# A spectral filter plus a gated layer on one core: a new order, new engines and new PSUM banks for 998 planned tasks

## The chip, the cores and the metric

The kernel runs on one core of one Trainium2 chip. The metric is the device time of one launch in microseconds. The core has five engines with an instruction stream each: PE (TensorE, matmuls; its weight loads are listed as PEld), DVE (VectorE), ACT (ScalarE), POOL (GpSimd) and SP (SyncE, which here only issues DMAs). Each stream runs in its own order, and streams meet at semaphores.

## The reference

```python
def reference(A_x, A_w_r, A_w_i, B_x, B_w_gate, B_w_up, B_w_down):
    def _A_ref(x, w_r, w_i):                    # x (1, 2048, 640)
        X = rfft2(x.astype(float32), axes=(-2, -1))
        X = X * (w_r + 1j * w_i)                # (2048, 321)
        return irfft2(X, s=(S, D), axes=(-2, -1)).astype(bfloat16)
    def _B_ref(x, w_gate, w_up, w_down):        # (640, 1536) twice, (1536, 640)
        g = einsum("bsd,df->bsf", x, w_gate)
        u = einsum("bsd,df->bsf", x, w_up)
        return einsum("bsf,fd->bsd", g * u, w_down)
    xn = _layernorm(A_x, axis=-1)
    return A_x + _A_ref(xn, A_w_r, A_w_i) + _B_ref(xn, B_w_gate, B_w_up, B_w_down)
```

All arrays are bf16. So the output is the input, plus a two-dimensional Fourier filter of the normalized input, plus a bilinear gated layer (GLU) of it.

## The kernel before

The kernel is a list of 998 tasks. A task has a name, the engines that may run it, a planned duration for each, and a function that emits its instructions. `_PLAN` (L403) is a written-out table of triples: task number, engine (0 PE, 1 ACT, 2 DVE, 3 POOL, 4 SP) and, for a PE task that opens PSUM space, its first bank of eight. `replay` (L151) walks the table in order, gives each task to its engine's stream, and makes whoever takes a bank depend on the tasks that emptied it. `compute_waits` (L196) turns dependences into semaphore waits. The durations in the code enter only into the planned clock that `replay` keeps; the emitted program is set by the table's order, engines and banks. A task's instruction waits at the head of its engine's stream, and everything behind it on that engine waits too.

The work has three stages.

Stage A normalizes the 16 row blocks (bn, ag, sd, rs, mul or sm, sq), transposes them (T0 on PE for the first four blocks, with evictions eT0; DMA transposes xt for the others), runs the first GLU groups (GU, L945 and L965, five matmuls of 512 columns each, or ten narrower ones in the first), and makes a first transform on DVE (S1 to S5) and PE (R, L905, evicted by eR). Every GU pair is evicted to bf16 (eG, L688 on ACT or L689 on DVE) and multiplied on DVE (H, L981). The buffer between eG and H has three slots.

Stage B carries the spectrum for t = 0 to 15 while the remaining GLU groups run beside it:

- D_t_0 and D_t_1 (PE, L1021) read the first transform. eD copies each result from PSUM as two copies of 64 partitions, one of which crosses to the other partition half.
- C_t (PE, L1041) is two matmuls of 321 columns into a pair of banks.
- WM_t (DVE, L1058 and L1061) multiplies C's result by the filter, six instructions, 256 columns four times and 130 columns twice.
- For every odd t, SM_t (DVE, L1074 and L1075) adds products across the partition halves; JA_t and JB_t (L689/L688 and L1086/L1085) copy or negate its halves across.
- A small side branch does the same for the columns divisible by five: X5A (L1096 on POOL or DVE, L1095 on ACT) and X5B, then the sum S5M (L1105), then J5A and J5B (L1117 is J5B's negation).
- IA (PE, L1132), four for every odd t, read all of SM, JA, JB and S5M, J5A, J5B of that t. eIA evicts them.

Stage C turns back: I (PE, L1160) needs all IA, eI evicts it, V1 to V5 (DVE) finish the inverse transform for a group of rows. ACC (PE, L1237) accumulates the GLU's down projection in PSUM, IV (PE, L1249) adds the inverse transform into the same bank, FINA (ACT) evicts, FIN (DVE) adds the input, and st_out stores.

Four functions show what the moved tasks do:

```python
def copy_on(c, dst, src):                                   # L686
    if c.e is nc.scalar:
        return c.e.activation(dst, src, _ACTF.Copy)
    return c.e.tensor_copy(dst, src)
...
def em_sm(c, lr=lr):                                        # L1072
    pa_, pb_ = v_pr[:, 0], v_pr[:, 1]
    c.e.tensor_tensor(v_l[0:64, lr, :, 0, :], pa_[0:64], pb_[64:128], _OP.subtract)
    return c.e.tensor_tensor(v_l[64:128, lr, :, 0, :], pa_[64:128], pb_[0:64], _OP.add)
...
def em_x5b(c):
    return copy_on(c, v_x5[64:128, :, 0:65], v_y5[0:64, 1, :, 0:65])
...
def em_s5(c, lr=lr):                                        # L1104
    return c.e.tensor_tensor(v_l5[:, lr, :, 0:65], v_y5[:, 0, :, 0:65], v_x5[:, :, 0:65], _OP.add)
```

Of the kernel before, what the change touches and what calls it, by code (L numbers as in the profile page):

```python
# [398 lines left out]
def _d_act(n):  # L399
    return n * 0.833 + 62.0  # L400
# [3 lines left out]
    (11, 4, -1), (0, 1, -1), (12, 4, -1), (170, 1, -1), (169, 4, -1), (17, 2, -1), (171, 4, -1), (8, 3, -1), (18, 2, -1),  # L404
    (19, 2, -1), (26, 2, -1), (20, 1, -1), (172, 4, -1), (21, 2, -1), (22, 2, -1), (10, 0, 0), (27, 2, -1), (28, 2, -1),
    (29, 1, -1), (23, 0, 2), (24, 1, -1), (25, 2, -1), (9, 0, 4), (30, 2, -1), (31, 2, -1), (181, 0, 5), (13, 4, -1),
    (32, 0, 6), (34, 2, -1), (33, 1, -1), (179, 0, 4), (189, 0, 0), (186, 0, 1), (14, 4, -1), (182, 2, -1), (36, 2, -1),
    (184, 0, 5), (191, 0, 2), (180, 1, -1), (35, 2, -1), (37, 2, -1), (183, 2, -1), (173, 4, -1), (187, 2, -1), (43, 1, -1),
    (38, 1, -1), (174, 4, -1), (196, 0, 3), (44, 1, -1), (45, 1, -1), (39, 2, -1), (194, 0, 4), (185, 2, -1), (175, 4, -1),
    (190, 1, -1), (40, 2, -1), (192, 1, -1), (41, 0, 5), (195, 1, -1), (188, 2, -1), (46, 2, -1), (47, 2, -1), (197, 1, -1),  # L410
    (112, 2, -1), (42, 1, -1), (201, 0, 6), (193, 2, -1), (176, 4, -1), (15, 4, -1), (113, 2, -1), (48, 0, 7), (198, 2, -1),
    (199, 0, 1), (49, 1, -1), (114, 2, -1), (177, 4, -1), (178, 4, -1), (206, 0, 0), (204, 0, 7), (50, 2, -1), (1, 4, -1),
    (53, 2, -1), (202, 1, -1), (211, 0, 6), (200, 1, -1), (207, 1, -1), (203, 2, -1), (51, 2, -1), (16, 4, -1), (62, 1, -1),
    (63, 1, -1), (54, 2, -1), (52, 2, -1), (55, 2, -1), (212, 1, -1), (2, 4, -1), (205, 1, -1), (56, 1, -1), (115, 2, -1),
    (3, 4, -1), (208, 2, -1), (209, 0, 2), (57, 2, -1), (210, 1, -1), (216, 0, 4), (64, 1, -1), (116, 2, -1), (214, 0, 5),
    (65, 1, -1), (4, 4, -1), (221, 0, 3), (5, 4, -1), (58, 2, -1), (217, 1, -1), (213, 2, -1), (121, 2, -1), (219, 0, 2),
    (119, 0, 0), (6, 4, -1), (226, 0, 4), (66, 1, -1), (215, 1, -1), (222, 1, -1), (7, 4, -1), (67, 2, -1), (218, 2, -1),
    (117, 0, 6), (122, 2, -1), (60, 2, -1), (59, 4, -1), (224, 0, 5), (220, 1, -1), (68, 2, -1), (72, 1, -1), (123, 2, -1),
    (223, 2, -1), (229, 0, 3), (124, 2, -1), (73, 1, -1), (70, 2, -1), (74, 1, -1), (227, 1, -1), (61, 4, -1), (75, 1, -1),
    (225, 1, -1), (125, 2, -1), (76, 1, -1), (231, 0, 2), (77, 2, -1), (234, 0, 4), (232, 1, -1), (230, 1, -1), (236, 0, 5),  # L420
    (120, 1, -1), (126, 0, 2), (69, 4, -1), (228, 2, -1), (71, 4, -1), (239, 0, 0), (78, 2, -1), (118, 1, -1), (237, 1, -1),
    (79, 4, -1), (82, 1, -1), (80, 2, -1), (233, 2, -1), (130, 2, -1), (128, 0, 6), (235, 1, -1), (81, 4, -1), (83, 1, -1),
    (241, 0, 1), (238, 2, -1), (131, 2, -1), (244, 0, 5), (240, 1, -1), (246, 0, 4), (431, 4, -1), (84, 1, -1), (249, 0, 0),
    (242, 1, -1), (243, 2, -1), (432, 4, -1), (251, 0, 1), (85, 1, -1), (132, 2, -1), (247, 1, -1), (433, 4, -1), (92, 1, -1),
    (254, 0, 4), (245, 1, -1), (256, 0, 5), (252, 1, -1), (86, 1, -1), (248, 2, -1), (87, 2, -1), (250, 1, -1), (434, 4, -1),
    (93, 1, -1), (257, 1, -1), (94, 1, -1), (133, 2, -1), (255, 1, -1), (95, 1, -1), (253, 2, -1), (90, 2, -1), (259, 0, 1),
    (261, 0, 0), (435, 4, -1), (134, 2, -1), (266, 0, 5), (258, 2, -1), (96, 1, -1), (97, 2, -1), (262, 1, -1), (260, 1, -1),
    (264, 0, 4), (88, 2, -1), (98, 2, -1), (129, 1, -1), (269, 0, 0), (137, 0, 6), (271, 0, 1), (127, 1, -1), (436, 4, -1),
    (100, 2, -1), (135, 0, 2), (267, 1, -1), (270, 1, -1), (263, 2, -1), (437, 4, -1), (438, 4, -1), (102, 1, -1), (274, 0, 5),
    (265, 1, -1), (138, 1, -1), (439, 4, -1), (440, 4, -1), (276, 0, 0), (272, 1, -1), (143, 2, -1), (268, 2, -1), (275, 1, -1),  # L430
    (103, 1, -1), (144, 2, -1), (141, 0, 6), (139, 0, 4), (277, 1, -1), (281, 0, 1), (136, 1, -1), (282, 1, -1), (279, 0, 0),
    (273, 2, -1), (104, 1, -1), (145, 2, -1), (278, 2, -1), (286, 0, 1), (105, 1, -1), (284, 0, 2), (287, 1, -1), (146, 2, -1),
    (280, 1, -1), (106, 1, -1), (283, 2, -1), (140, 1, -1), (289, 0, 3), (291, 0, 1), (107, 2, -1), (294, 0, 0), (285, 1, -1),
    (296, 0, 2), (290, 1, -1), (441, 4, -1), (147, 2, -1), (292, 1, -1), (442, 4, -1), (148, 0, 4), (471, 4, -1), (142, 1, -1),
    (110, 2, -1), (288, 2, -1), (150, 0, 6), (472, 4, -1), (295, 1, -1), (108, 2, -1), (301, 0, 3), (293, 2, -1), (473, 4, -1),
    (89, 4, -1), (154, 0, 0), (297, 1, -1), (299, 0, 2), (302, 1, -1), (156, 2, -1), (91, 4, -1), (99, 4, -1), (298, 2, -1),
    (149, 1, -1), (157, 2, -1), (101, 4, -1), (151, 1, -1), (300, 1, -1), (306, 0, 3), (474, 4, -1), (303, 2, -1), (152, 0, 4),
    (304, 0, 2), (307, 1, -1), (153, 1, -1), (311, 0, 3), (305, 1, -1), (158, 2, -1), (309, 0, 2), (475, 4, -1), (155, 1, -1),
    (310, 1, -1), (308, 2, -1), (312, 1, -1), (476, 4, -1), (316, 0, 6), (159, 2, -1), (317, 1, -1), (477, 4, -1), (160, 2, -1),
    (319, 0, 7), (478, 4, -1), (313, 2, -1), (314, 0, 6), (167, 0, 4), (161, 0, 0), (320, 1, -1), (168, 1, -1), (315, 2, -1),  # L440
    (162, 2, -1), (163, 0, 2), (165, 0, 6), (164, 2, -1), (321, 0, 4), (166, 1, -1), (318, 2, -1), (445, 0, 5), (109, 4, -1),
    (446, 2, -1), (322, 1, -1), (111, 4, -1), (443, 0, 0), (451, 0, 1), (449, 0, 6), (429, 4, -1), (430, 4, -1), (723, 4, -1),
    (323, 2, -1), (444, 1, -1), (324, 0, 7), (450, 1, -1), (479, 0, 0), (724, 4, -1), (325, 1, -1), (447, 0, 2), (326, 0, 4),
    (480, 1, -1), (452, 2, -1), (507, 4, -1), (453, 0, 6), (485, 0, 5), (448, 2, -1), (329, 0, 1), (487, 0, 0), (481, 0, 2),
    (327, 1, -1), (334, 0, 4), (486, 1, -1), (331, 0, 3), (454, 2, -1), (488, 1, -1), (508, 4, -1), (459, 3, -1), (330, 1, -1),
    (458, 1, -1), (328, 2, -1), (515, 0, 5), (517, 0, 0), (455, 2, -1), (482, 1, -1), (336, 0, 1), (460, 3, -1), (335, 1, -1),
    (489, 0, 6), (509, 4, -1), (516, 2, -1), (553, 0, 2), (332, 1, -1), (333, 2, -1), (483, 0, 4), (337, 1, -1), (490, 2, -1),
    (339, 0, 3), (484, 2, -1), (554, 1, -1), (510, 4, -1), (511, 4, -1), (457, 1, -1), (344, 0, 1), (461, 3, -1), (341, 0, 2),
    (338, 2, -1), (521, 0, 6), (491, 2, -1), (340, 1, -1), (494, 3, -1), (518, 1, -1), (345, 1, -1), (523, 0, 7), (342, 1, -1),
    (346, 0, 3), (495, 1, -1), (343, 2, -1), (524, 1, -1), (496, 3, -1), (512, 4, -1), (492, 2, -1), (462, 3, -1), (513, 4, -1),  # L450
    (456, 2, -1), (498, 3, -1), (522, 1, -1), (551, 0, 2), (514, 4, -1), (543, 4, -1), (349, 0, 0), (519, 0, 4), (354, 0, 1),
    (347, 1, -1), (525, 0, 6), (552, 1, -1), (493, 1, -1), (520, 2, -1), (497, 3, -1), (469, 0, 3), (544, 4, -1), (356, 0, 2),
    (526, 2, -1), (355, 1, -1), (531, 3, -1), (348, 2, -1), (350, 1, -1), (545, 4, -1), (351, 0, 4), (499, 0, 5), (465, 0, 1),
    (357, 1, -1), (589, 0, 0), (557, 0, 2), (467, 0, 6), (470, 1, -1), (352, 1, -1), (558, 1, -1), (463, 0, 7), (546, 4, -1),
    (503, 0, 4), (361, 0, 3), (547, 4, -1), (500, 1, -1), (548, 4, -1), (530, 3, -1), (549, 4, -1), (559, 0, 2), (359, 0, 5),
    (550, 4, -1), (468, 1, -1), (532, 3, -1), (590, 2, -1), (353, 2, -1), (579, 4, -1), (527, 2, -1), (580, 4, -1), (466, 1, -1),
    (501, 0, 6), (560, 1, -1), (555, 0, 0), (364, 0, 2), (362, 1, -1), (504, 1, -1), (534, 3, -1), (358, 2, -1), (581, 4, -1),
# [66 lines left out]
def _build(nc, A_x, A_w_r, A_w_i, B_w_gate, B_w_up, B_w_down, out, opts=None):  # L524
# [3 lines left out]
    with es:  # L528
# [49 lines left out]
        b_pr = alloc("PR", 2048)  # L578
# [92 lines left out]
        T = sch.task  # L671
# [60 lines left out]
        for gi, (b0, nb) in enumerate(_LN_GROUPS):  # L732
            pbase = 1.0 + 0.05 * gi if gi < 4 else opts.get("ln_prio", 5.9) + 0.05 * (gi - opts.get("ln_lead", 3))
            for b in range(b0, b0 + nb):
                if b in aset:
# [9 lines left out]
                    def em_sq(c, b=b):  # L745
# [3 lines left out]
                      reads=[(b_x, ("s", b, b + 1)), (b_m32, ("b", b, b + 1))],  # L749
# [611 lines left out]
```

## Time and profile before

| what | value |
|---|---|
| median of 8 runs | 200.58 us (200.39 to 201.18) |
| the profiled execution's own time | 200.47 us |
| its span, first to last instruction | 198.7 us |
| granted TensorE clock | 1.0 throughout |
| busy share of the span | PE 97%, DVE 91%, ACT 72%, POOL 12% |
| instructions | PE 1593 matmuls, DVE 394, ACT 307, POOL 35 |
| first and last work | first LayerNorm statistics 3.32 us, last addition 196.43 us |

Times inside the execution are microseconds from the span's start. In a row of the groups, "busy" is the sum over the group and the next number the mean duration in ns. An instruction's duration includes the tail in which the next one already runs, so two neighbours may start closer together than the duration: where a start-to-start distance is meant, the text says so. A busy PE is not a PE at its peak.

### The profile page before, as it was taken

What the parts mean: (1) busy time and instruction counts of PE and PEld (TensorE: products, weight loads), DVE (VectorE), ACT (ScalarE), POOL (GpSimd) and SP (SyncE); (2) the same over time, 40 slices, a digit from 0 to 9 for tenths busy, and PEclk for the clock granted to TensorE, in tenths of its full rate; (3) what the DMA queues carried; (4) which work ended last, traced back from release to release, by engine and by line L of the source; (5) the groups of instructions that cost most, each with busy time, mean ns of one, the idle gap of its engine ahead of it and who ended that gap; (6) DMA issues with size and microseconds to landing.
All of it is one profiled execution on the core that took longest, in us unless ns stands there. A gap on an engine that the chain in (4) does not pass through costs nothing.

```text
span 198.7 us, 4239 instructions
## 1 busy us (share of the span) xinstructions
PE 192.6 (97%) x1593; PEld 122.3 (62%) x1593; DVE 180.6 (91%) x394; ACT 142.1 (72%) x307; POOL 23.1 (12%) x35
## 2 busy tenths in 40 slices
PE   8899999999999999899899999999999999999995
PEld 8798645445455555455455555457777777777774
DVE  3799999999999999999999999997999998999653
ACT  3398999999969589999898999998414431543220
POOL 0000000000000003184353442320000000000000
PEclk9999999999999999999999999999999999999999
DMA  6999995417327441442332400205101235033412
GB/s 184 306 330 376 387 163 115 126 35 109 95 47 228 163 115 46 108 113 63 96 88 58 122 0 3 68 0 147 54 3 47 85 102 162 36 132 102 132 68 68
DMA packets 29652, 23.26 MB, mean 117 GB/s; under 512 B 10560, under 2 KB 27584, under 8 KB 29504
## 3 DMA queue, kind: packets, MB, share of 16 engines
q1 hardware_dynamic: 28832, 22.64, 41.5%
q10 hardware_dynamic: 800, 0.36, 0.6%
q8 instruction: 12, 0.20, 0.5%
q14 instruction: 8, 0.07, 0.1%
HBM read 18.40 MB, written 2.62 MB: 106 GB/s over the span
## 4 chain that ended last, share of the span: by engine, by line
PE 77%; ACT 13%; DVE 6%; issue 1%; DMA 1%
PE ps L945 33%; PE ps L1237 26%; ACT arena L688 12%; PE ps L965 7%; PE ps L905 2%; PE ps L1160 2%; PE ps L1249 2%; DVE arena L1058 2%; PE ps L1132 1%; PE ps L1021 1%; DMA arena<-in_A_x_dram 1%; PE ps L1041 1%; DVE arena L689 1%; DVE arena L755 1%; DVE arena L981 1%
## 5 line engine op out<-in xcount | busy, mean ns | idle before, releaser
L688 ACT ACTIVATE arena<-ps 128x512 bf16<-128x512 f32 (+7 forms) x241 | 116.0, 531 | 46.1 <-PE ps L1249 24.6
L945 PE MATMUL ps<-arena 128*128 128x512 bf16 x420 | 98.2, 379 | 0.1
L945 PEld LDWEIGHTS ps<-arena 128*128 128x128 bf16 x420 | 38.6, 98 | 40.7 <-ACT arena L688 0.6
L1237 PE MATMUL ps<-arena 128*128 128x320 bf16 (+2 forms) x396 | 57.2, 295 | 0.0
L1237 PEld LDWEIGHTS ps<-arena 128*128 128x128 bf16 x396 | 37.6, 98 | 13.2
L1058 DVE TENSOR_TENSOR arena<-ps,arena 128x256 bf16<-128x256 f32 x64 | 22.6, 414 | 0.2
L981 DVE TENSOR_TENSOR arena<-arena 128x512 bf16<-128x512 bf16 x42 | 18.4, 440 | 0.4
L689 POOL COPY arena<-arena 64x252 bf16<-64x252 bf16 (+1 forms) x13 | 6.3, 487 | 92.3 <-DVE arena L1061 91.0
L965 PE MATMUL ps<-arena 128*128 128x128 bf16 (+1 forms) x160 | 14.0, 246 | 0.5 <-ACT arena L688 0.5
L965 PEld LDWEIGHTS ps<-arena 128*128 128x128 bf16 x160 | 12.3, 98 | 1.6 <-issue 0.6
L1276 DVE TENSOR_TENSOR arena<-arena 128x640 bf16<-128x640 bf16 x15 | 7.2, 489 | 6.2 <-ACT arena L688 5.9
L689 DVE CAST arena<-ps 64x321 bf16<-64x321 f32 (+4 forms) x20 | 10.6, 549 | 0.9 <-PE ps L945 0.4
L1021 PEld LDWEIGHTS ps<-arena 128*128 128x128 bf16 x160 | 7.4, 98 | 4.0 <-issue 0.4
L746 ACT ACTIVATE arena<-arena 128x640 bf16<-128x640 bf16 x11 | 9.3, 842 | 0.1
L1132 PEld LDWEIGHTS ps<-arena 128*128 128x128 bf16 x160 | 7.7, 116 | 2.5
L1041 PE MATMUL ps<-arena 128*128 128x321 bf16 x32 | 7.0, 300 | 2.0 <-ACT arena L688 1.2
L737 ACT ACTIVATE arena<-arena 128x640 bf16<-128x640 bf16 x11 | 8.3, 752 | 0.7 <-DMA arena<-in_A_x_dram 0.6
L1132 PE MATMUL ps<-arena 128*128 128x64 bf16 x160 | 8.6, 198 | 0.0
L1021 PE MATMUL ps<-arena 128*128 128x64 bf16 (+1 forms) x160 | 8.4, 193 | 0.0
L1249 PE MATMUL ps<-arena 128*128 128x320 bf16 (+2 forms) x33 | 8.1, 295 | 0.0
L1061 DVE TENSOR_TENSOR arena<-ps,arena 128x130 bf16<-128x130 f32 x32 | 7.9, 289 | 0.0
L857 DVE TENSOR_TENSOR arena<-arena 128x768 f32<-128x768 bf16 (+1 forms) x10 | 7.9, 790 | 0.0
(66 smaller groups left out, 199.3 us busy)
## 6 DMA issues: line engine op xcount, KB each, us to landing
arena<-in_A_x_dram SPq DMA_DIRECT2D x20, 160.0 KB, 2.6
arena<-in_A_w_r_dram SPq DMA_DIRECT2D x30, 80.2 KB, 2.2
arena<-in_A_w_i_dram SPq DMA_DIRECT2D x30, 80.2 KB, 2.2
out_dram<-arena SPq DMA_DIRECT2D x15, 160.0 KB, 1.8
arena<-in_B_w_gate_dram SPq DMA_DIRECT2D x4, 320.0 KB, 5.3
arena<-in_A_x_dram SPq DMA_DIRECT2D x1, 1280.0 KB, 9.9
arena<-in_B_w_down_dram SPq DMA_DIRECT2D x2, 640.0 KB, 7.1
arena<-c_tf SPq DMA_DIRECT2D x4, 256.0 KB, 10.1
```

The lines of the kernel that those rows point to most:

```text
L688: return c.e.activation(dst, src, _ACTF.Copy)
L689: return c.e.tensor_copy(dst, src)
L746: return c.e.activation(v_jk, v_x[:, b, :], _ACTF.Square, scale=-1.0, bias=v_m32[:, b:b + 1], accum_out=v_ss[:, b:b + 1])
L945: ins = c.e.matmul(ps[:, bk, :], v_gw[:, w, j, ft, :], v_xt[:, j, rows], start=(j == 0), stop=(j == 4))
L965: ins = c.e.matmul(ps[:, bk, w * n:(w + 1) * n], v_gw[:, w, j, ft, :], v_xt[:, j, rows], start=(j == 0), stop=(j == 4))
L981: return c.e.tensor_tensor(v_ht[:, ft0, rows], v_gbf[:, rr, 0, :], v_gbf[:, rr, 1, :], _OP.mult)
L1021: ins = c.e.matmul(ps[:, bk, k * 64:k * 64 + n], v_uq[:, k, t, :], v_fd[:, k * 128 + w * n: k * 128 + w * n + n], start=True, stop=True)
L1041: ins = c.e.matmul(ps[:, bank_of(c.t) + g, 0:_LP], v_tf[:, 2 * t + g, :], v_a[:, ar, 324 * g:324 * g + _LP], start=True, stop=True)
L1058: c.e.tensor_tensor(dst, xh, wv, _OP.mult)
L1132: ins = c.e.matmul(ps[:, bk, 64 * k:64 * k + 64], st, v_ti[:, q, :], start=True, stop=True)
L1237: ins = c.e.matmul(ps[:, bk, 0:sl3.stop - sl3.start], v_ht[:, ft, a * 128:(a + 1) * 128], v_wd[:, ft, sl3], start=(ft == _FT_ORDER[0]), st ...
L1249: return c.e.matmul(ps[:, bank_of(own), 0:sl3.stop - sl3.start], v_sm[:, 2, :], v_v[:, a, sl3], start=False, stop=True)
```

## The change

The whole table is replaced. The tasks, their instructions and their operands are the same 998; their order on PE, ACT, DVE and POOL, the engine of 31 of them, and the first bank of 213 of the 251 tasks that open PSUM space differ. SP's list and the two loads on ACT's queue stay as they were, in the same order.

In the code two kinds of lines differ: the table, of which two lines are shown here, and the planned durations.

```diff
-    (11, 4, -1), (0, 1, -1), (12, 4, -1), (170, 1, -1), (169, 4, -1), (17, 2, -1), (171, 4, -1), (8, 3, -1), (18, 2, -1),
...
+    (984, 2, -1), (994, 0, -1), (990, 2, -1), (985, 4, -1), (995, 0, -1), (991, 4, -1), (996, 2, -1), (997, 4, -1),
...
-                ed = T("eD_%d_%d" % (t, w), ("act", "dve"), {"dve": 910.0, "act": 880.0},
+                ed = T("eD_%d_%d" % (t, w), ("act", "dve"), {"dve": 1032.0, "act": 906.0},
...
-            wm = T("WM_%d" % t, "dve", 1862.0, em_wm,
+            wm = T("WM_%d" % t, "dve", 1800.0, em_wm,
...
-            T("SM_%d" % t, "dve", 1420.0, em_sm, reads=[(b_pr, ("r", 0, 2))],
+            T("SM_%d" % t, "dve", 1520.0, em_sm, reads=[(b_pr, ("r", 0, 2))],
...
-                T("%s_%d" % (nm, t), ("act", "dve"), {"act": _d_act(1024) + 70.0, "dve": 454.0}, em,
+                T("%s_%d" % (nm, t), ("act", "dve"), {"act": 1079.0, "dve": 500.0}, em,
...
-                T("%s_%d" % (nm, t), ("pool", "act", "dve"), {"pool": 950.0, "act": _d_act(260) + 20.0, "dve": 330.0}, em,
+                T("%s_%d" % (nm, t), ("pool", "act", "dve"), {"pool": (1250.0, 760.0)[i_], "act": 445.0, "dve": 330.0}, em,
...
-            T("S5M_%d" % t, ("pool", "dve"), {"pool": 900.0, "dve": 204.0}, em_s5,
+            T("S5M_%d" % t, ("pool", "dve"), {"pool": 1450.0, "dve": 332.0}, em_s5,
...
-                T("%s_%d" % (nm, t), ("pool", "act", "dve"), {"pool": 900.0, "act": _d_act(252) + 20.0, "dve": 330.0}, em,
+                T("%s_%d" % (nm, t), ("pool", "act", "dve"), {"pool": (620.0, 1240.0)[i_ - 1], "act": 440.0, "dve": 330.0}, em,
```

With names in place of numbers, the tasks that change engine are these.

| task | before to after |
|---|---|
| eT0_1_act, eR_14, eG_28_0 | ACT to DVE |
| eR_12, eR_13, eG_0_1, eG_27_0 | DVE to ACT |
| eD_4_0 | DVE to ACT |
| eG_43_0; eG_43_1, eG_47_0 | ACT to DVE; DVE to ACT |
| JB_1, JB_13 | ACT to DVE |
| X5A_1, X5B_11 | ACT to DVE |
| X5A_5 | POOL to DVE |
| X5A_3, X5A_9 | POOL to ACT |
| X5B_3, X5B_15 | ACT to POOL |
| S5M_9, S5M_13; S5M_15 | DVE to POOL; POOL to DVE |
| J5B_15 | DVE to ACT |
| eIA_25, eIA_28; eIA_30 | ACT to DVE; DVE to ACT |
| eI_0, eI_1, eI_11; eI_2 | ACT to DVE; DVE to ACT |

The order changes throughout. The places that matter for reading on are the starts of PE's and DVE's lists and the end of DVE's list in stage B:

```
PE  before: warm T0_0 fill GU_1_0 T0_1 GU_0_0 GU_0_1 GU_3_0 ...
PE  after:  warm T0_0 fill T0_1 GU_1_0 GU_0_0 GU_1_1 GU_3_0 ...
DVE before: bn0_0 bn0_1 ag0 bn1_0 rs_0 mul0 bn1_1 ag1 eT0_0_dve rs_1 mul1 eT0_1_dve eG_0_1 ...
DVE after:  bn0_1 bn0_0 bn1_1 ag0 bn1_0 rs_0 ag1 mul0 rs_1 mul1 eT0_0_dve eT0_1_dve eT0_1_act ...
DVE before, end of stage B: WM_15 WM_14 H_46 SM_15 JB_15 J5B_15 JA_15 eG_47_0 eIA_30 eIA_31 eG_48_1 eI_2 H_47 V1_0
DVE after,  end of stage B: WM_15 H_45 WM_14 H_46 SM_15 S5M_15 JA_15 JB_15 eIA_25 eIA_28 eIA_31 eG_48_1 eI_1 H_47 eI_0 V1_0
PE  before, end of stage B: GU_11_12_1 IA_30 IA_29 IA_31 IA_28 ACC_0_0_0
PE  after,  end of stage B: GU_11_12_0 IA_28 IA_29 IA_31 IA_30 ACC_0_0_0
```

On ACT the new list has `eIA_26 eIA_21 X5A_15 eG_47_0 eIA_24 J5B_15 eIA_27` near the end of stage B. The last eleven PE tasks are the same in both tables.

## The prediction

> **What bounds the kernel now.** I read the page's busy line and chain first, then busy time in windows, then the waits in one window, then single rows. The page points at two engines:
>
> ```profile
> PE 192.6 (97%) x1593; PEld 122.3 (62%) x1593; DVE 180.6 (91%) x394; ACT 142.1 (72%) x307; POOL 23.1 (12%) x35
> PE 77%; ACT 13%; DVE 6%; issue 1%; DMA 1%
> ```
>
> PE is busy and carries 77% of the chain, but 13% runs over ACT and 6% over DVE, so there is a stretch where PE follows. The chain in order of time puts it between 80 and 121 us. There are three stages. A, to 71.2 us: GLU matmuls and the first transforms. B, 71.2 to 135.1: D, C, WM, SM, JA/JB, IA beside 42 GLU groups. C, from 135.1: ACC, I, V, IV. In A (from 8.5) and C PE works without a gap. Busy us in five windows of B, columns PE, PEld, DVE, ACT, POOL:
>
> ```profile
> 71.50:80.00 8.50, 8.41 (x82) 4.45 (x79) 8.23 (x21) 8.23 (x19) 2.04 (x3) 1.00 0.38 102
> 80.00:92.00 12.00, 11.27 (x82) 5.66 (x83) 11.78 (x32) 11.70 (x24) 4.52 (x6) 1.00 0.37 90
> 92.00:105.00 13.00, 11.81 (x126) 6.91 (x124) 12.65 (x31) 12.29 (x30) 6.88 (x9) 1.00 0.38 96
> 105.00:121.00 16.00, 16.00 (x141) 8.57 (x139) 15.64 (x42) 15.17 (x34) 6.22 (x8) 1.00 0.19 48
> 121.00:134.00 13.00, 12.90 (x117) 6.84 (x116) 12.68 (x36) 12.75 (x29) 3.14 (x5) 1.00 0.10 27
> ```
>
> DVE and ACT are both near 97%. Which leads? The waits inside 71.5 to 134 us (total, times, longest), asked by engine:
>
> ```profile
> DVE arena L689 <- PE ps L1021: 0.2, 1, 0.2
> ACT arena L688 <- PE ps L945: 0.8, 2, 0.4
> ACT arena L688 <- PE ps L1021: 0.4, 1, 0.4
> PE ps L1041 <- ACT arena L688: 1.2, 2, 0.7
> PE ps L1041 <- DVE arena L689: 0.5, 1, 0.5
> ```
>
> DVE waits for others 0.2 us in 62.5. ACT and PE wait for it or for each other. So B is as long as DVE's own list, and PE's stalls there are the consequence. Their size: 42 groups x 1.079 us (start to start) + 16 C x 0.272 + 32 D x 0.145 + 32 IA x 0.166 = 59.6 us of PE work, against 135.09 - 71.22 = 63.9, so 4.2 us of stall. DVE's last item in B gates its end:
>
> ```profile
> 133.52 0.42 DVE L689 COPY arena<-arena 64x1024 bf16<-64x1024 bf16 x1
> 134.38 0.88 PE L1132 MATMUL ps<-arena 128*128 128x64 bf16 x20
> ```
>
> JA_15 ends at 133.94; the last four IA could start 0.15 us later (mul0 to T0_0 took that), at 134.09, and start at 134.38: 0.29 us to spare.
>
> **The change, part by part.** *Start.* DVE gets bn1_1 ahead of ag0 (start to start 0.41 us), so mul0 and T0_0 come 0.4 later. But T0_1 then runs before the first GLU group instead of after it, and PE's 0.15 us wait for eT0_1 ahead of the group at 8.49 is gone. Walked through: the later eT0 evictions end 6.89, the first group starts 7.14 instead of 6.95, yet without T0_1's 0.28 and the 0.15 behind it the third group starts 8.26 instead of 8.49: -0.2 us. In A, H_26 stands behind the same DVE work in both lists, and R_12 becomes ready as before. eR_12 and eR_13 go to ACT, eR_14 to DVE: three ACT evictions 0.58 apart end at about 70.85, and D_0_1 starts at 71.0 instead of 71.22. I take -0.2; ends 0 (A's DVE eats it) and -0.25. mul6 and mul7 swap, so xt6 and xt7 are issued up to 3 us later and land by about 33; their first reader stands at 35.
>
> *DVE's list in B.* Counting kinds from eD_0_1 to the last JA/JB: eD 4 to 3, JB 5 to 7, X5A 1 to 3, X5B 0 to 1, S5M 2 to 1, J5B 1 to 0; WM 16, SM 8, H 19, JA 6, eIA 1 and eG 1 stay. DVE rows of this window (count, busy us, mean ns):
>
> ```profile
> L689 DVE CAST arena<-ps 64x321 bf16<-64x321 f32 x8 | 3.9, 493 | 0.3 <-PE ps L1021 0.2
> L1086 DVE TENSOR_SCALAR arena<-arena 64x1024 bf16<-64x1024 bf16 x5 | 2.7, 545 | 0.2
> L1105 DVE TENSOR_TENSOR arena<-arena 128x260 bf16<-128x260 bf16 x2 | 0.6, 300 | 0.1
> L1117 DVE TENSOR_SCALAR arena<-arena 64x252 bf16<-64x252 bf16 x1 | 0.4, 415 | 0.0
> L1096 DVE TENSOR_SCALAR arena<-arena 64x260 bf16<-64x260 bf16 x1 | 0.2, 228 | 0.0
> ```
>
> An eD is two CASTs: -0.99. Two JB +1.09, three X5 copies +0.68 (X5B by X5A's row), S5M -0.30, J5B -0.42: +0.07 us. Orders within the list change the 0.1 us breaks between neighbours: about +-0.3.
>
> *S5M on POOL, 6 to 7.* The trace shows what this does to DVE:
>
> ```profile
> 101.87 0.69 DVE L1074 TENSOR_TENSOR arena<-arena 64x1024 bf16<-64x1024 bf16 x1
> 102.57 1.08 DVE L1075 TENSOR_TENSOR arena<-arena 64x1024 bf16<-64x1024 bf16 x1
> 101.92 1.18 POOL L1105 TENSOR_TENSOR arena<-arena 128x260 bf16<-128x260 bf16 x1 [0.63 <-PE ps L945]
> 131.57 0.69 DVE L1075 TENSOR_TENSOR arena<-arena 64x1024 bf16<-64x1024 bf16 x1
> ```
>
> SM's second half takes 1.08 beside POOL's sum and 0.69 alone. At all six sums one DVE instruction (SM_1, H_32, SM_5, SM_7, H_42, JB_15) is 0.30 to 0.44 us longer than its like, 0.38 in the mean. One more sum on POOL: +0.38; ends 0 (it falls beside a WM, which reads PSUM) and, should two fall away so, -0.8. POOL's copies cost DVE little: SM's first half took 0.78 beside the X5A at 85.1 us, 0.09 more than alone.
>
> [...]
>
> *ACT.* In B: JB 3 to 1, X5A 3 to 4, X5B 3 to 0, J5B 0 to 1, eD 28 to 29, eG +1, eIA -1: -2 x 1.06 + 0.42 - 1.26 + 0.42 + 0.87 + 0.60 - 0.44 = -1.5 us. I cost it at nothing: DVE, which waited 0.2 us in all, hides it; if DVE's cover is gone, it is the first rival's price.
>
> *New waits on ACT.* X5A_3, 9, 13 and 15 stand in ACT's list and wait for the second WM of their pair; J5B_15 waits for S5M_15. Adding up ACT's and DVE's lists from the first eD (start-to-start times of the trace by neighbours), ACT reaches X5A_3 0.2 us, X5A_9 0.8, X5A_13 1.3 and X5A_15 1.4 us before WM has ended. Behind them stand eG_33_0 and eG_32_0, eG_39_0, eD_15_0, and eG_47_0, so the products H_32 and H_39 on DVE and PE's banks wait as long. By the same sums H_32 still finds its eviction 1.7 us early and C_9, C_13 and C_15 end 3.6 to 4.0 us ahead of their WM (2.1 to 3.4 in the old list), so I charge DVE nothing; the ends are 0 and 1.4 us, the longest of these waits passed on whole.
>
> *Stage C.* The same matmuls, 61 us. V1_0 needs eI_0 to eI_3, two of them now on DVE: still 3.4 us behind the first ACC (3.5 before). V5_0 ends about 13.7 us behind it, and 14.9 us of ACC and I stand ahead of IV_0_1 (14.5 before), so nothing waits. The later V5 have over 2 us each. H_48 and H_49 come earlier, eI_11 costs DVE 0.8: hidden by the same slack. The last eleven PE tasks and the order of DMAs stay. 0. Banks: 213 of 251 differ, but none's next user comes before its eviction by these sums.
>
> *Sum.* JB_15 ends at 133.94 - 0.2 + 0.07 + 0.38 = 134.2, IA starts at 134.34 against 134.38: -0.04, and about 0.07 less wait between the last eIA and the first I. So -0.1 us: the profiled execution's 200.47 (span 198.7 and 1.8 around it) becomes 200.4, and the median, 0.11 above it, **200.5**.
>
> **Rivals.** *ACT leads B, and the stalls dissolve.* The chain runs over ACT from 92 to 121 us, and ACT loses 1.5 us; C's eviction no longer comes late (PE waited 0.9 us for C_6, 0.6 for C_8, both behind ACT). Then B shrinks by 1.5 and the start by 0.2: 198.9. Against it: DVE's 0.2 us. It needs DVE's stretched instructions to shrink too.
>
> *DVE begins to wait (slower).* S5M_15 now stands on DVE directly ahead of JA_15 and JB_15, and needs X5A_15, which ACT makes behind eIA_26 and eIA_21. POOL waited for such an X5A (L1095) 4.8 us in two waits. By the sums X5A_15 ends near 131.8 and DVE arrives near 132.3: it decides once ACT or PE runs more than 0.5 us later, and then costs one for one. At 1.7 us late, 1.2 us: 201.7. DVE has never had another engine's copy in front of the stage's last items; the old list had S5M_15 on POOL.
>
> *The change does nothing measurable* is the forecast itself, not a third case.
>
> **How the numbers follow.** A measurement of this kernel tells about 0.2% (0.4 us) from no change. Forecast, within 0.4 us: 0.38. ACT rival 0.28, and 0.05 for fewer stretched DVE instructions: faster 0.33. DVE waits 0.24, and 0.05 for a stall in A's or C's new order: slower 0.29. The range goes from the ACT rival's 198.9, less 0.1, to the waiting rival at 201.6; the forecast's own range is 200.0 to 201.0 (the +-0.3 of order and one S5M).
>
> **What would show it.** Right: DVE waits under 0.5 us in B, B 63.5 to 64.3 us from the first D to the first ACC, PE stalls about 4 us but elsewhere, seven DVE instructions 0.3 to 0.44 us long beside L1105 on POOL, first D at 71.0, no PE gap in C. Wrong: B under 63 us, with SM, H and JA unstretched, or DVE waiting for ACT L1095 or L688 for a microsecond.

## The result, and the profile after

The changed kernel takes **201.50 us** in the median (201.43 to 202.21), the kernel before, on the same chip, 200.54 us (200.34 to 201.18). The ratio is **1.0046, with a 95% interval of 1.0036 to 1.0057**: 0.7 to 1.1 us slower. The forecast was 200.5 us, no change.

The page of the changed kernel has these two lines, busy time and chain by engine:

```profile
PE 193.3 (97%) x1593; PEld 122.5 (61%) x1593; DVE 181.8 (91%) x396; ACT 139.4 (70%) x305; POOL 24.2 (12%) x35
PE 61%; DVE 21%; ACT 7%; SPq 4%; DMA 4%; issue 2%
```

ACT has 2.7 us less work, DVE 1.2 us more, and DVE's share of the chain went from 6% to 21%. Busy time in the same five windows of stage B (columns PE, PEld, DVE, ACT, POOL, then clock, DMA share, GB/s):

```profile
71.50:80.00 8.50, 8.50 (x84) 4.74 (x85) 8.02 (x21) 8.21 (x19) 2.28 (x3) 1.00 0.36 96
80.00:92.00 12.00, 11.12 (x77) 5.33 (x76) 11.77 (x32) 10.98 (x23) 3.89 (x6) 1.00 0.39 97
92.00:105.00 13.00, 12.19 (x133) 7.30 (x132) 12.55 (x30) 12.53 (x30) 6.09 (x8) 1.00 0.35 93
105.00:121.00 16.00, 15.50 (x130) 7.98 (x128) 15.66 (x41) 14.66 (x32) 6.34 (x8) 1.00 0.19 50
121.00:134.00 13.00, 12.66 (x111) 6.88 (x110) 12.76 (x34) 11.70 (x27) 4.61 (x6) 1.00 0.09 27
```

ACT now has air (11.70 of 13.00 in the last window, 12.75 before). DVE is as full as it was. The waits of 71.5 to 134 us (total, times, longest):

```profile
PE ps L1041 <- DVE arena L1075: 1.4, 3, 0.6
...
ACT arena L688 <- PE ps L945: 1.3, 4, 0.5
...
DVE arena L689 <- PE ps L1021: 0.6, 1, 0.6
...
PE ps L1041 <- ACT arena L688: 0.3, 1, 0.3
```

DVE's one wait stands ahead of its first eD. From there to its last JA or JB it waits for nobody. C on PE now waits mainly for SM (L1075), where before it waited for ACT (1.2) and for a DVE copy (0.5). Stage by stage, from the first D and the first ACC of each profile: A ends at 71.44 (71.23 before), B lasts 64.89 (63.86), C 61.23 (61.30). So the loss lies in B. DVE's own list there, from eD_0_1 to the start of what follows the last JA or JB, grew from 62.29 to 63.59 us.

### The profile page after: what moved, and what is told of

Read it like the earlier page. It is cut to its first block, busy times and chain, and to the rows that moved or that the text cites. A ratio compares the mean times of both kernels' runs of the same rounds, so it can differ in the third digit from the quotient of the medians.

```text
span 199.8 us, 4237 instructions
## 1 busy us (share of the span) xinstructions
PE 193.3 (97%) x1593; PEld 122.5 (61%) x1593; DVE 181.8 (91%) x396; ACT 139.4 (70%) x305; POOL 24.2 (12%) x35
## 4 chain that ended last, share of the span: by engine, by line
PE 61%; DVE 21%; ACT 7%; SPq 4%; DMA 4%; issue 2%
PE ps L945 27%; PE ps L1237 26%; DVE arena L1058 8%; ACT arena L688 4%; SPq L682 4%; DMA arena<-in_A_x_dram 4%; DVE arena L981 3%; DVE arena L689 3%; DVE arena L1061 3%; DVE arena L1075 2%; PE ps L1160 2%; PE ps L1249 2%; PE ps L905 2%; DVE arena L1074 1%; PE ps L1132 1%
## 5 line engine op out<-in xcount | busy, mean ns | idle before, releaser
L689 POOL COPY arena<-arena 64x252 bf16<-64x252 bf16 (+1 forms) x15 | 8.7, 583 | 102.2 <-DVE arena L1061 100.1
L689 DVE CAST arena<-ps 64x321 bf16<-64x321 f32 (+4 forms) x16 | 8.4, 540 | 1.1 <-PE ps L1021 0.6
L755 DVE BATCH_NORM_STATS2 arena<-arena 128x6 f32<-128x320 bf16 x10 | 4.3, 480 | 4.8 <-DMA arena<-in_A_x_dram 4.8
```

## Where DVE's 1.30 us come from

Each DVE instruction was set against the duration that its kind has with nothing beside it (SM's halves 0.69, H 0.415, JA and JB 0.42, S5M 0.30, X5 0.228, J5B 0.415), and each break, the start of the next instruction less the end of this one, was added up.

| us of DVE's list in B | before | after | difference |
|---|---|---|---|
| bare durations | 59.24 | 59.05 | -0.19 |
| long stretches, 0.36 to 0.45 each, beside POOL's S5M | 2.35 (6) | 2.64 (7) | +0.29 |
| other stretches, 0.08 to 0.19 each, beside POOL's copies and negations (X5, J5) | 1.42 (14) | 2.01 (19) | +0.59 |
| rest | 0.09 | 0.12 | +0.03 |
| breaks between tasks | -0.81 | -0.23 | +0.58 |
| sum | 62.29 | 63.59 | +1.30 |

Of the other stretches, those beside an X5 went from 6 to 8 (0.54 to 0.82 us) and those beside J5 alone from 8 to 11 (0.88 to 1.20 us). The stretches show in the groups of B. DVE rows (count, busy us, mean ns), first before, then after:

```profile
L981 DVE TENSOR_TENSOR arena<-arena 128x512 bf16<-128x512 bf16 x19 | 8.9, 472 | 0.3
...
L1075 DVE TENSOR_TENSOR arena<-arena 64x1024 bf16<-64x1024 bf16 x8 | 6.5, 809 | 0.1
L1074 DVE TENSOR_TENSOR arena<-arena 64x1024 bf16<-64x1024 bf16 x8 | 6.2, 778 | 0.3
```

```profile
L981 DVE TENSOR_TENSOR arena<-arena 128x512 bf16<-128x512 bf16 x19 | 8.6, 453 | 0.4
...
L1074 DVE TENSOR_TENSOR arena<-arena 64x1024 bf16<-64x1024 bf16 x8 | 7.2, 896 | 0.2
L1075 DVE TENSOR_TENSOR arena<-arena 64x1024 bf16<-64x1024 bf16 x8 | 7.1, 884 | 0.1
```

SM's two lines together take 1.6 us more for the same sixteen instructions, H 0.3 less. POOL's rows of J5B and J5A show the other side of the meeting; before, then after:

```profile
L1117 POOL TENSOR_SCALAR arena<-arena 64x252 bf16<-64x252 bf16 x7 | 7.1, 1009 | 2.2 <-DVE arena L1105 1.7
...
L689 POOL COPY arena<-arena 64x252 bf16<-64x252 bf16 x8 | 3.7, 459 | 1.4 <-DVE arena L1105 0.9
```

```profile
L1117 POOL TENSOR_SCALAR arena<-arena 64x252 bf16<-64x252 bf16 x7 | 7.6, 1084 | 0.6
...
L689 POOL COPY arena<-arena 64x252 bf16<-64x252 bf16 x8 | 5.0, 631 | 2.1 <-DVE arena L1105 1.6
```

The same copies got longer: more of them now meet DVE work that stretches them. What a meeting looks like shows in one pair, t = 3, in order of time. Before, DVE (SM_3's halves, H_32, JA_3 and JA_1), then POOL (X5A_3, S5M_3, J5B_1 and J5B_3):

```profile
85.33 0.78 DVE L1074 TENSOR_TENSOR arena<-arena 64x1024 bf16<-64x1024 bf16 x1
86.12 0.69 DVE L1075 TENSOR_TENSOR arena<-arena 64x1024 bf16<-64x1024 bf16 x1
86.84 0.79 DVE L981 TENSOR_TENSOR arena<-arena 128x512 bf16<-128x512 bf16 x1
87.66 1.03 DVE L689 COPY arena<-arena 64x1024 bf16<-64x1024 bf16 x2
```

```profile
85.06 0.96 POOL L1096 TENSOR_SCALAR arena<-arena 64x260 bf16<-64x260 bf16 x1 [4.92 <-DVE arena L1061]
86.17 1.18 POOL L1105 TENSOR_TENSOR arena<-arena 128x260 bf16<-128x260 bf16 x1
87.43 1.94 POOL L1117 TENSOR_SCALAR arena<-arena 64x252 bf16<-64x252 bf16 x2
```

After, DVE (SM_3's halves, H_32), then POOL (S5M_3, J5B_3, J5A_3):

```profile
85.81 1.06 DVE L1074 TENSOR_TENSOR arena<-arena 64x1024 bf16<-64x1024 bf16 x1
86.89 0.79 DVE L1075 TENSOR_TENSOR arena<-arena 64x1024 bf16<-64x1024 bf16 x1
87.71 0.60 DVE L981 TENSOR_TENSOR arena<-arena 128x512 bf16<-128x512 bf16 x1
```

```profile
85.65 0.68 POOL L1105 TENSOR_TENSOR arena<-arena 128x260 bf16<-128x260 bf16 x1
86.42 1.16 POOL L1117 TENSOR_SCALAR arena<-arena 64x252 bf16<-64x252 bf16 x1
87.64 0.39 POOL L689 COPY arena<-arena 64x252 bf16<-64x252 bf16 x1
```

The sum costs 0.37 in both (H_32 before, SM's first half after). After, J5B adds 0.10 to SM's second half and J5A 0.19 to H_32. Before, J5B_1 and J5B_3 added 0.08 to JA_3 and 0.19 to JA_1, and most of the rest of their time lay beside WM. So this pair shows the price of a meeting and not the loss: in the whole of B five more DVE instructions meet a copy, two more at t = 1 and 3 taken together, two more at 13, two more at 15, one more at 7 and two fewer at 9.

## The experiments

Stage A's end scatters between executions of the same kernel (the first D of nine profiles with stage A as changed stood at 71.12 to 71.79), so a profile tells more by the length of B, which for one and the same list repeats to 0.04 us (64.89, 64.92, 64.93). "Long" and "other" are the two kinds of stretches of the table above.

| run | ratio to before, 95% | median us | B us | DVE list us | long (count) | other |
|---|---|---|---|---|---|---|
| before | | 200.54 | 63.86 | 62.29 | 2.35 (6) | 1.42 |
| after | 1.0046 (1.0036 to 1.0057) | 201.50 | 64.89 | 63.59 | 2.64 (7) | 2.01 |
| a_before_b_after | 1.0051 (1.0038 to 1.0064) | 201.69 | 64.93 | 63.61 | 2.64 (7) | 2.01 |
| a_after_b_before | 1.0008 (0.9989 to 1.0027) | 200.83 | 63.90 | 62.33 | 2.40 (6) | 1.43 |
| eg7_first | 1.0032 (1.0017 to 1.0047) | 201.30 | 64.92 | 63.62 | 2.65 (7) | 2.01 |
| s5_on_dve | 0.9951 (0.9936 to 0.9966) | 199.67 | 63.00 | 61.77 | 0 | 1.62 |
| s5_double | 1.0140 (1.0120 to 1.0161) | 203.45 | 66.61 | 65.34 | 4.57 (12) | 1.89 |
| s5_late | 1.0378 (1.0361 to 1.0396) | 208.25 | 71.52 | 70.07 | 0 | 0.91 |
| old_s5_on_dve | 0.9960 (0.9945 to 0.9975) | 199.73 | 63.10 | 61.30 | 0 | 1.56 |
| s5_on_dve_eg7 | 0.9936 (0.9922 to 0.9950) | 199.39 | 63.01 | 61.78 | 0 | 1.62 |
| j5_late | 1.0016 (0.9998 to 1.0033) | 200.93 | 63.87 | 62.55 | 2.64 (7) | 0.91 |
| dose_beside_wm | 1.0014 (0.9998 to 1.0030) | 200.77 | 63.88 | 62.73 | 2.64 (7) | 1.08 |
| x5a_on_pool | 1.0052 (1.0032 to 1.0071) | 201.70 | 64.42 | 63.12 | 2.41 (6) | 2.02 |
| s5_dve_j5_late | 0.9904 (0.9882 to 0.9926) | 198.69 | 62.41 | 61.11 | 0 | 0.91 |
| ja_after_sm | 1.0072 (1.0048 to 1.0097) | 202.23 | 65.33 | 63.50 | 2.67 (7) | 1.86 |
| best_ja_s5 | 0.9923 (0.9896 to 0.9950) | 199.10 | 62.64 | 61.31 | 0 | 0.90 |
| hold_dose | 0.9930 (0.9900 to 0.9960) | 199.62 | 62.98 | 61.51 | 0 | 0.70 |
| hold_less | 0.9914 (0.9885 to 0.9944) | 198.84 | 62.27 | 60.97 | 0 | 0.90 |

Runs that were made together share a chip; on the chips of this table the kernel before has medians of 200.54 to 201.06 us, so the ratios are to be compared, not the medians.

**Which stage.** Stage A of one table, stages B and C of the other.

```diff
# a_before_b_after: tasks up to the first D as before, the rest as changed
# a_after_b_before: the reverse
```

> Stage A (all tasks up to the first D) in the order, engines and banks of before, stages B and C as changed. If the change's two parts are separate, the first D comes 0.2 us earlier than in the changed kernel and B takes 64.9 us: 201.2 to 201.4 us. Rival (the longer B comes from how A hands over, its late first D and busy ACT): B back to 63.9 us, 200.4 to 200.6 us.

> Stage A as changed, stages B and C in the order, engines and banks of before. Separate parts: the first D 0.2 us later, B 63.9 us, 200.6 to 200.9 us. Rival (the hand-over from A sets B): 201.3 to 201.6 us.

B is 64.93 with the new B and 63.90 with the old one, whatever A was. The whole loss is in B, and A does not hand it over. A's own share is lost in its scatter.

**The stall in A.** The new list makes PE wait in A, where it had not waited. In the changed kernel's order of time (start, us, engine, idle before):

```profile
23.01 2.32 PE L945 MATMUL ps<-arena 128*128 128x512 bf16 x10 [0.26 <-ACT arena L688]
```

This is GU_6_0_0, whose bank eG_7_1 frees; eG_7_1 stood on ACT behind sq7. By matmul starts the gap is 0.43 us.

```diff
-ACT: sq7 eG_7_1
+ACT: eG_7_1 sq7
```

> The changed kernel with one ACT task moved: eG_7_1 ahead of sq7 in stage A, so that the PSUM bank of GU_6_0_0 comes free earlier. Theory: PE's stall of 0.43 us at GU_6_0_0 goes, the first D starts 0.3 to 0.45 us earlier, 201.05 to 201.2 us. Rival (sq7 comes 0.6 us later, and the normalization of block 7 and what hangs on it holds something else up, or DVE's work in A sets the first D): 201.4 to 201.7 us.

GU_6_0_0 begins 0.46 us earlier in the profile and B is unchanged. The time is 0.2 us less than the changed kernel's, less than expected, and the two intervals overlap. The profiles say the same: six of them have this edit, and their first D stands at 71.09 in the median, against 71.29 with the stall and 71.23 in the old order. By these medians the opening gains some 0.15 us and the stall eats it. Each group scatters by 0.2 to 0.7 us, so this is likely and not shown.

**The sums, taken away.**

```diff
-POOL: X5B_1 S5M_1 J5A_1 J5B_1 ...
+POOL: X5B_1 J5A_1 J5B_1 ...
-DVE: SM_1 H_29 ...
+DVE: SM_1 S5M_1 H_29 ...          # so for t = 1 to 13; S5M_15 is there already
```

> The changed kernel with all eight S5M on DVE, each directly behind SM_t, and none on POOL. Contention theory (stage B is as long as DVE's own list, and each POOL sum makes the SM half beside it 0.39 to 0.48 us longer): per sum DVE gains 0.39 to 0.48 us and pays 0.2 to 0.3 us for doing the sum itself; seven sums make -0.6 to -1.9 us, so 199.6 to 200.9 us, all SM at 1.4 to 1.5 us. Rival (the longer B is a matter of order: PE and ACT lead, DVE only follows): DVE gets seven instructions of 0.2 to 0.3 us more and nothing shrinks that matters, 201.5 to 203 us.

```profile
L1074 DVE TENSOR_TENSOR arena<-arena 64x1024 bf16<-64x1024 bf16 x8 | 5.9, 736 | 0.2
L1075 DVE TENSOR_TENSOR arena<-arena 64x1024 bf16<-64x1024 bf16 x8 | 5.5, 687 | 0.1
...
L1105 DVE TENSOR_TENSOR arena<-arena 128x260 bf16<-128x260 bf16 x8 | 2.4, 300 | 0.2
```

These are its DVE rows in B: seven more instructions on DVE, and its list is 1.8 us shorter. SM lost 2.9 us, and the seven moved sums cost 0.21 each from start to start. This kernel is faster than the kernel before, while the rival (order alone) expected the sums to cost time.

**The sums, doubled.** Each S5M on POOL is preceded by the same sum into unused space.

```diff
+                if c.e is nc.gpsimd:
+                    c.e.tensor_tensor(v_dm[:, :, 0:65], v_y5[:, 0, :, 0:65], v_x5[:, :, 0:65], _OP.add)
                 return c.e.tensor_tensor(v_l5[:, lr, :, 0:65], ...)
```

> The changed kernel with each S5M on POOL made twice (the same sum goes to unused space first): a second dose of POOL's sum, with nothing else on any engine. Contention theory: seven more DVE instructions are stretched by about 0.4 us each, B is 2.5 to 3 us longer, 204 to 204.5 us. Rival (POOL's work is hidden): POOL has time to spare, at most +0.3 us, 201.5 to 201.8 us.

B is 1.72 us longer, all of it in DVE's list, with no instruction more on DVE, ACT or PE. The dose was two thirds of what I expected: five more long stretches, not seven.

**The sums, held back.** One extra dependence for each S5M.

```diff
+        for a, b in (("S5M_1", "H_30"), ("S5M_3", "H_33"), ("S5M_5", "JA_5"), ...):
+            by[a].deps.add(by[b])
```

> The changed kernel with every S5M still on POOL, but held back by one extra dependence until the DVE task just ahead of the next WM has run, so that the sum runs beside WM, which reads PSUM, and not beside SM; J5B_9 moves behind J5A_9 on POOL. DVE's list is the same. Contention theory: SM goes back from 1.8 to about 1.47 us, DVE's list in B is 2.5 to 3 us shorter, B 62 to 62.5 us instead of 64.9, time 198.6 to 199.2 us; if WM is stretched as SM was, 201 to 202. Rival (order, not contention, is what is slow): the later J5 and IA make it the same or slower, 201.5 to 202.5 us.

```profile
PE ps L1041 <- POOL arena L1105: 8.8, 6, 1.8
```

```profile
DVE arena L1058 <- PE ps L1041: 9.7, 7, 1.4
```

The experiment did not do what it was made for. WM overwrites the products that S5M reads, and the code lets C start only when its WM may start, so PE's next C waited for the late sum (first line) and DVE for that C (second). A sum of one pair can't lie beside the next WM. SM itself went back to 0.71 and 0.69 us in the mean, with no sum and no J5 on POOL beside it.

**The sums of the kernel before.**

```diff
-POOL: S5M_1 S5M_3 S5M_5 S5M_7 S5M_11 S5M_15
+DVE: SM_t S5M_t                   # for these six t
```

> The kernel before (its order, engines and banks) with its six POOL sums S5M_1, 3, 5, 7, 11 and 15 moved to DVE, each directly behind SM_t, where S5M_13 stands already. Contention theory: six stretches of 0.38 us in the mean go (-2.3), six sums of 0.23 us start to start come (+1.4): 199.4 to 199.8 us. Rival (the gain seen in the changed kernel comes from some other weakness of its order, and the order before had none to give back): DVE's list grows by the sums, 200.5 to 202 us.

199.73: the old order, too, paid for its POOL sums, nearly 0.4% of the time.

> The changed kernel with both mends at once: all S5M on DVE directly behind SM_t (alone 199.67 us), and eG_7_1 ahead of sq7 on ACT (alone -0.2 us). If the two lie in different stages and add, 199.4 to 199.5 us. Rival (the start gained in stage A is lost again, because in stage B something other than DVE's list now ends last): 199.6 to 199.7 us.

This kernel joins the edits of s5_on_dve and eg7_first, and both hold.

**The copies.** The edit has the form of s5_late's, on the J5 pair, which WM does not overwrite.

```diff
-POOL: ... J5A_9 X5A_11 S5M_11 J5B_9
+POOL: ... J5A_9 J5B_9 X5A_11 S5M_11
+        for a, b in (("J5A_1", "H_30"), ("J5B_3", "H_33"), ("J5B_5", "JA_5"), ("J5A_7", "JB_7"),
+                     ("J5A_9", "H_40"), ("J5A_11", "H_42"), ("J5A_13", "JB_13")):
+            by[a].deps.add(by[b])
```

> The changed kernel with one thing altered: on POOL, J5A_t and J5B_t are held by an extra dependence until the DVE task just ahead of the next WM has run, so these copies of 64 partitions run beside WM (which reads PSUM) and not beside SM, H, JA and JB; J5B_9 moves behind J5A_9. S5M stays where it is. IA, the reader of J5, comes 1.9 us or more after that. Theory (small stretches of 0.08 to 0.2 us, which I had left out of the sum, make up a good part of the longer DVE list): about 1.0 to 1.4 us of them go, 200.1 to 200.6 us. Rival (only the sums count): 201.3 to 201.7 us, or more if an IA comes late.

```profile
L1117 POOL TENSOR_SCALAR arena<-arena 64x252 bf16<-64x252 bf16 x7 | 5.8, 835 | 5.4 <-DVE arena L981 2.7 <-DVE arena L689 2.2
...
L689 POOL COPY arena<-arena 64x252 bf16<-64x252 bf16 x8 | 3.4, 424 | 12.5 <-DVE arena L981 6.3 <-DVE arena L1086 4.4 <-DVE arena L1105 1.6
```

Beside WM the same POOL copies take 0.84 and 0.42 us instead of 1.08 and 0.63, and DVE's other stretches fall from 2.01 to 0.91. B is back to 63.87, the length it had before the change, though the seven sums are still on POOL. The time, 200.93, is above what was expected: by the ratios 0.6 us less than the changed kernel (give or take 0.4), where B lost 1.02. In that profile A ended late (71.79); whether that is all of the difference stays open.

**A dose where it should cost nothing.** The kernel of j5_late with seven sums more on POOL, behind the last J5 of each t.

```diff
+                    if t.name in _DOSE:
+                        eng.wait_ge(sems[("eng", "pool")], t.seq)
+                        eng.tensor_tensor(v_dm[:, :, 0:65], v_dm[:, :, 0:65], v_dm[:, :, 0:65], _OP.add).then_inc(s_dm, 1)
+                        eng.wait_ge(s_dm, _DOSE.index(t.name) + 1)
```

> The kernel of j5_late with seven further sums of S5M's shape on POOL, in unused space, one right behind the last J5 of each t, so that they run beside the WM pair. Theory (a POOL sum stretches only DVE instructions whose data are all in SBUF; WM took 1.82 to 1.86 us in every run, beside POOL or not): the same time as j5_late within 0.3 us, all WM at 1.8 to 1.9 us. Rival (any POOL sum costs DVE 0.38 us, wherever it falls): 2.5 to 2.8 us more than j5_late.

The seven sums, from POOL's groups, and WM's large instructions, from DVE's groups in B (all lines are shifted by the insertion):

```profile
L1317 POOL TENSOR_TENSOR dm<-dm 128x260 bf16<-128x260 bf16 x7 | 4.3, 621 | 0.6
```

```profile
L1060 DVE TENSOR_TENSOR arena<-ps,arena 128x256 bf16<-128x256 f32 x64 | 22.6, 416 | 0.1
```

B is 63.88 against 63.87. Of the 64 large WM instructions 38 now lie beside POOL work (28 in j5_late), and take 0.416 us in the mean, the other 26 as well. A sum of the shape that costs DVE 0.38 beside SM costs it nothing beside WM.

**Is it the X5A?** The change took X5A_3, 5 and 9 off POOL.

```diff
-ACT: X5A_3 X5A_9          DVE: X5A_5
+POOL: X5B_3 X5A_3 S5M_3   X5B_5 X5A_5 S5M_5   X5B_9 X5A_9 S5M_9
```

> The changed kernel with X5A_3, X5A_5 and X5A_9 back on POOL, each behind X5B_t, as POOL had them before. Theory (taking these copies off POOL let its sums and J5 start earlier, beside SM): for these three t the sum falls later, on H or JA, and J5 beside WM; DVE also loses X5A_5; 200.8 to 201.3 us. Rival (the next C has to wait for the late sum, and WM for that C): 201.7 to 203 us, with DVE waiting for PE L1041.

Mixed. DVE's list is 0.47 us shorter (X5A_5 gone, one long stretch fewer) and B with it, but the other stretches stay at 2.02: those beside J5 alone fall from 1.20 to 1.03 us, and those beside X5 rise from 0.82 to 0.99. So it was not these three moves alone that brought J5 beside SM; and the timed runs show no gain over the changed kernel. Which of the moves brought J5 there stays open.

**Both together.** The edits of s5_on_dve_eg7 and j5_late.

> All S5M on DVE behind SM_t, eG_7_1 ahead of sq7 (those two together: 199.39 us), and in addition J5A and J5B held on POOL until they run beside WM. Theory: the small stretches beside J5 go, some 0.6 to 0.8 us in this kernel, 198.6 to 198.9 us. Rival (by now ACT or PE ends last in stage B): 199.3 to 199.6 us.

198.69 us: 1.0% less than before (0.7 to 1.2%), with every stretch beside a sum or a J5 gone but J5A_15's.

**The breaks.** Six tasks moved within DVE's list of the changed kernel.

```diff
-DVE: SM_1 H_29 JA_1 H_30 WM_2     SM_5 H_35 JA_5 WM_7     SM_7 H_37 JB_7 WM_8
+DVE: SM_1 JA_1 H_29 H_30 WM_2     SM_5 JA_5 H_35 WM_7     SM_7 JB_7 H_37 WM_8
# likewise JA_3, JA_9 and JB_13
```

> The changed kernel with six tasks moved within DVE's list: JA_1, JA_3, JA_5, JB_7, JA_9 and JB_13 directly behind SM_t, ahead of the H that stood between. Same tasks, same engines; only neighbours differ. Theory (a break between neighbours is +0.03 us or -0.08 us by the pair: H to JA, JA to H and JA to WM +0.03, H to H and H to WM -0.08): each move turns one +0.03 into -0.08, six make -0.66 us, 200.8 to 201.1 us. Rival (breaks come from something else, or the later H holds PE and ACT up): 201.4 to 202 us.

```profile
PE ps L945 <- DVE arena L981: 1.3, 3, 0.6
```

A miss. An H directly behind an H had to wait for its input (breaks of 0.10), so the breaks did not shrink (-0.23 to -0.21), and PE, which had never waited for H in B, now waited 1.3 us for the later H. DVE's list fell by 0.09 and B rose by 0.44: here PE, not DVE, ended last.

> The kernel of s5_dve_j5_late with JA_1, JA_3 and JA_9 directly behind SM_t, ahead of S5M_t, so that S5M, H, H and WM follow one another. Theory of the pair: three breaks of +0.03 become -0.08 us, 198.3 to 198.5 us. Rival (S5M 0.45 us later holds the next C, and WM for it): 198.7 to 199.3 us.

The same edit for JA_1, JA_3 and JA_9 in the kernel of s5_dve_j5_late, with the same outcome: B 62.64 instead of 62.41.

So a break does not go by the kinds of two neighbours. It goes by where they start. Every operand in SBUF here starts at partition 0 or 64. I went through DVE's list of B in both traces and marked each task with an operand in SBUF or PSUM that starts elsewhere than the first input (for a read) or the output (for a write) of the last instruction to read or write there. Two rows of the kernel before, WM's last two instructions and H_31, and the row at 85.33 shown above, SM_3's first half, have one break of each kind:

```profile
84.47 0.49 DVE L1061 TENSOR_TENSOR arena<-ps,arena 128x130 bf16<-128x130 f32 x2
84.88 0.42 DVE L981 TENSOR_TENSOR arena<-arena 128x512 bf16<-128x512 bf16 x1
```

H_31 starts from partition 0 like WM and begins 0.08 us before WM's end. SM's half also reads from 64, and begins 0.03 us after H_31's end. Before, 37 of 64 breaks follow such a change, after, 46 of 66. All 83 are positive (82 times 0.03, once 0.05). Of the other 47, 46 are negative (mostly -0.08); the one exception, +0.10, is an H at 126.55 in the kernel before that waited for its input, an eviction that ended on ACT at 126.38. The 183 breaks inside tasks go the same way (0.01 at the 23 with such a change, about -0.08 at the other 160). Nine more changes (+0.26 us) and seven fewer of the other breaks (+0.32) make the table's +0.58. So in the two traces every break but that one goes by the start; what makes the difference is in no view. Two runs test it, on the kernel of s5_dve_j5_late and not on the changed kernel itself.

```diff
# hold_dose
-DVE: H_28 X5A_1 SM_1    H_31 JB_1 SM_3    H_41 JB_9 X5B_11    H_43 JA_11 JB_11
+DVE: X5A_1 H_28 SM_1    JB_1 H_31 SM_3    JB_9 H_41 X5B_11    JA_11 H_43 JB_11
# hold_less
-DVE: WM_6 JB_5 X5A_7 H_36 SM_7
+DVE: WM_6 H_36 JB_5 X5A_7 SM_7
```

> The kernel of s5_dve_j5_late with four swaps of neighbours on DVE: X5A_1 ahead of H_28, JB_1 ahead of H_31, JB_9 ahead of H_41, JA_11 ahead of H_43. Theory of the start partition: in the traces of before and after, a break is -0.08 us where an instruction reads and writes SBUF from the same partition halves as those ahead of it, and +0.03 us where a half changes; the swaps put an H (from partition 0) between instructions that start at 64 on one side, five more changes of half, 5 x 0.11 = 0.55 us: DVE's list in B and the time 0.5 to 0.6 us longer, 199.2 to 199.3 us. Rival (breaks are not set so; the swaps only reorder): 198.6 to 198.8 us, unless H held back makes PE wait. [...]

> The kernel of s5_dve_j5_late with one swap on DVE: H_36 ahead of JB_5 and X5A_7 instead of behind them. Theory of the start partition: one change of half fewer, DVE's list in B 0.11 us shorter, which is seen in the length of stage B (it repeats to 0.05 us between executions) rather than in the time: B 62.3 instead of 62.41 us, 198.55 to 198.65 us. Rival: B the same, or longer, if the later JB_5 holds IA of t = 5 up.

hold_dose: five more breaks at a change of start (44 to 49), B 62.98 instead of 62.41. The breaks grew by 0.72 (one of those at a change, ahead of WM_15, is 0.13) and the rest of the list shrank by 0.32, mostly since the swapped tasks meet POOL's copies at other points (X5B_11 went from 0.42 to 0.23 us); PE's 0.9 us of waits for H add what the list does not show. hold_less: one such break fewer, list and B both 0.14 us shorter. Its time, 198.84, is not told apart from 198.69. Of the swaps, then, the sign and roughly the size of both agree.

## Why the prediction was wrong, step by step

- **B is as long as DVE's own list: right.** DVE waited 0.6 us, ahead of its first eD, and for nobody after that to the end of its list. Every run in which DVE's list changed by over 0.3 us moved B the same way by a similar amount (+1.30 and +1.03 here; -0.99 and -0.76 in old_s5_on_dve), apart from s5_late, where DVE itself waited. So PE's stalls in B (5.3 us after, 4.2 before) read as consequences. ja_after_sm shows where this ends: as soon as H comes half a microsecond later, PE leads (it waits 1.3 us for H, and B grows by 0.44).
- **ACT's relief costed at nothing: right.** ACT lost its work in B, and B grew. That the ACT rival needed stretched instructions to shrink as well was the right condition; they grew.
- **S5M on POOL, +0.38: right** in mechanism and size, +0.29 in the trace (seven long stretches of 0.38). The six before measure 0.37 to 0.44 us, not from 0.30.
- **"POOL's copies cost DVE little": this step failed.** It went by one row, 0.09 us beside X5A, and multiplied it by nothing. The traces have 14 such stretches beside POOL's X5 and J5 before and 19 after, 0.08 to 0.19 us each beside a copy or negation of 0.39 to 1.31 us, 1.42 and 2.01 us in all: +0.59 us that the sum did not hold. j5_late takes 1.10 of them away, and B shortens by 1.02.
- **"Breaks between neighbours: about +-0.3": this step failed in size.** The trace has +0.58. It could have been counted from the two lists before any run, since only the start partitions of the tasks enter.
- **Durations by kind, +0.07:** -0.19. The row of JB (545 ns) held stretches and so counted part of them twice. The bare 0.42 us of a JB gives the right figure.
- **Start, -0.2:** the transpose T0_2 did come 0.20 us earlier (11.64 for 11.84), but "none's next user comes before its eviction" failed at GU_6_0_0, 0.43 us. By the medians of the first D, 71.29 and 71.23, A is worth about nothing.
- **Stage C, 0: right** (61.23 against 61.30, without a gap).
- **The waiting rival did not occur:** S5M_15 began on DVE 0.03 us behind SM_15. It named the right sign and nearly the right time (201.7), but its mechanism is absent.

With the two failed terms at their measured size, the prediction's own sum gives -0.1 + 0.59 + 0.58 = +1.1 us, 201.6. That it comes so near the measured 201.5 is partly luck: the other terms were off as well, by -0.26 (durations), -0.09 (the sum on POOL) and about +0.26 (the start), and nearly cancel.

## What to carry to other kernels

Where one engine's list bounds a stage, cost not only the instructions on it but what runs beside each: here a sum on the helper engine cost nothing beside WM, which reads PSUM (0.416 us with POOL work and without), and 0.38 us in the mean beside SM and H, whose inputs all lie in SBUF, and holding J5 back until WM ran took 1.02 us out of B. Multiply a small cost by its count before calling it small. Count the places where a list changes the partitions it starts from: here each costs 0.11 us between tasks, and the count can be read off the code.

## What the runs showed of the hardware that was not expected

- In the two traces a POOL sum of 128x260 bf16 lengthens a DVE operation on two SBUF inputs by 0.36 to 0.40 us (JB_15, with one SBUF input, by 0.44) and takes 0.68 to 1.18 us itself; beside WM, which has one input in PSUM, DVE's large instructions take 0.416 us, as long as without POOL work (dose_beside_wm), and POOL's sum 0.68 us (s5_late) or 0.62 (dose_beside_wm).
- The DVE instruction that starts next pays. In all thirteen meetings the sum ends 0.54 to 0.62 us after the DVE instruction beside which it starts (twelve times 0.54 to 0.56, and never sooner than 0.68 after its own start), and the DVE instruction that starts next is the one that is stretched, by 0.36 to 0.45 us. Why is in no view.
- Sums cheaper on the busy engine: S5M costs POOL 0.93 us in the mean and DVE 0.38 through POOL, but only 0.21 us from start to start on DVE itself. Keeping this work off the bounding engine made that engine later.
- The break between two DVE tasks takes two values, 0.03 and about -0.08 us, by the partitions at which they start (127 of 130 in the two traces to within 0.02 us).
- The length of stage B repeats to 0.04 us between executions of the same list, while the start of it scatters by up to 0.7 us, so a profile resolves changes that the timed runs do not.
